# One chunk of a transformer block's attention sums its channel tiles further, with a new hand-written order and another place for late output tiles

## The chip, the cores and the metric

The kernel runs on one core of one Trainium2 chip. What counts is the device time of one execution in microseconds (us): 205.92 us is the median of three runs of the kernel before (205.92 to 206.48).

## What is computed

The reference normalizes `x` (2048 positions, 640 features, bf16) and adds to it an attention over a dilated window and a dense layer pair, both of the normalized `x`.

```python
def _A_ref(x, wqkv, wo):          # H = 32 heads of Dh = 20, W = 8, dil = 2
    qkv = (x @ wqkv).reshape(B, S, 3, H, Dh).transpose(2, 0, 3, 1, 4)
    q, k, v = qkv[0], qkv[1], qkv[2]
    idx = pos[:, None] - (jnp.arange(W) * dil)[None, :]
    mask = idx >= 0
    ...
    logits = jnp.einsum("bhsd,bhswd->bhsw", q, kg) * scale
    logits = jnp.where(mask[None, None, :, :], logits, -1e9)
    attn = _softmax(logits, axis=-1)
    o = jnp.einsum("bhsw,bhswd->bhsd", attn, vg)
    return o.transpose(0, 2, 1, 3).reshape(B, S, D) @ wo

def _B_ref(x, w1, b1, w2, b2):    # F = 1536
    h = _gelu(jnp.einsum("bsd,df->bsf", x, w1) + b1)
    return jnp.einsum("bsf,fd->bsd", h, w2) + b2

xn = _layernorm(x, axis=-1)
return x + _A_ref(xn, A_wqkv, A_wo) + _B_ref(xn, B_w1, B_b1, B_w2, B_b2)
```

Each position looks at itself and at seven positions before it, two apart. There are 32 heads with 20 channels each.

## The kernel before

The 2048 positions are four chunks (n = 0 to 3) of 512, each four blocks of 128 (j or bl = 0 to 3). The work is cut into named pieces, and `ORDER` (from line 42) is a list of their names, written out by hand: the pieces are issued in this order, and each engine executes its own in the order in which it meets them. No scheduler moves anything. A piece waits where its inputs, or the buffer it writes, are not ready; whatever is queued behind it on the same engine waits as well.

In the names the first digit is the chunk. The pieces of one chunk are:

- `st`, `rs`, `rc`, `xn`: statistics and normalization (`su`, `sq`, `ng` in chunks 2 and 3, where ScalarE makes the sums); `tc`: the normalized rows are transposed, from chunk 1 on by a transposing DMA on SyncE's queue (`do_td`, L295).
- `pj` and `pc`: projections to q, k and v by TensorE (L339) and their copies out of PSUM by ScalarE (L403). Chunk 0 has `ga`, `gd`, `hj` and `hc` instead. Two buffers serve the four chunks' v tiles, so a copy of chunk 2 waits until chunk 0 is done with its own.
- `qk` (L436): VectorE multiplies q with four shifted views of k, one half of the window at a time, 128 x 2560 elements. A partition holds one of four channel groups of one of 32 heads, and five channel tiles (t = 0 to 4) hold the rest.
- `pa` (L471): VectorE adds channel tiles: step 0 adds tiles 2 and 3 to tiles 0 and 1 (128 x 2048), step 1 adds tile 1 to tile 0, step 2 adds tile 4 to tile 0 (128 x 1024 each). `KEPT[n]` says how many tiles are left: 2 for chunk 0, where step 2 is left out, and 1 for the others.
- `lg` (L479): TensorE sums what is left over the four channel groups, with 32 output columns for each block, so that the four blocks' matmuls lie side by side in the array. These matmuls are called readers here, since they read what VectorE has made. There are 2 halves x 4 blocks x `KEPT[n]` of them.
- `cl`, `mask`, `m`, `mx`, `ex`, `ss`, `ri`, `at`: the softmax; `xd` (L554): its weights are broadcast by DMA, on SyncE's queue, to the four channel groups, one DMA for each block.
- `av` (L563): VectorE multiplies the shifted views of v with the weights; `aa` (L573): the two halves are added by a DMA with accumulation on GpSimd's queue (by VectorE, L575, in chunk 3); `ab` (L582) and `ot` (L586): the rest of the sum over the window, by VectorE.
- `f1` (L595) and `ge` (L611): first dense layer and GELU. In chunk 3 the results lie in the weights of q and k, which are spent by then (`do_ge`).
- `o` (L631 and L633): second dense layer (pieces 0 to 3) and the output projection of the attention (piece 4) into one pair of PSUM tiles, `lo` with 512 columns and `hi` with 128. `oc` (L638): ScalarE copies them to a tile `osb`, of which the pool `outp` has two. `od` (L644): a DMA on GpSimd's queue adds the tile to the output in DRAM.
- The output in DRAM first receives `x` (`xp`, SyncE's queue) and then the bias b2 (`xb`, GpSimd's queue, accumulating); an `od` waits until the `xb` of its chunk has landed. The very last block is finished otherwise (`oclo`, `ohi`, `ochi`, `ochd`): VectorE adds, and plain DMAs store.

Two lists name blocks whose `ab` or first `pa` would be done by a DMA (`AB_DMA`, `PA_DMA`); all their entries are empty.

Of the kernel before, what the change touches and what calls it, by code (L numbers as in the profile page):

```python
# [22 lines left out]
NCH = S // CH  # L23
BPC = CH // P
# [5 lines left out]
LASTB = S // P - 1  # L30
WARM = 10

KEPT = (2, 1, 1, 1)
BY_DMA = ((0, 1, 2, 3), (0, 1, 2, 3), (0, 1, 2, 3), ())
AB_DMA = ((), (), (), ())
PA_DMA = ((), (), (), ())
CUT = 2560
ACT_STATS = (2, 3)

# [3 lines left out]
wb st00a sum1 wa pad01 st00 rs00 ldx rc00 xn00a tp00a xn00b tp00b tc00a ga neg1 sq1 rs01 rc01 tc00b gb2 mean1 xn01  # L43
tp01 gb3 gb4 tc01a gd tc01b ho ge gc1 st03a st03 rs03 gc0 hj102 rc03 hc102 tb b1 hj101 hc101 st02a st02 rs02 hj100
hc100 xn03 tp03 tc03 pk hj202 rc02 xn02 tp02 tc02 gc4 hj201 hc201 hj111 st11a st10a hc111 st12a hj012 hc012 st11 hc202
st13a st13 hj112 hc112 st10 st12 rs1 qk010 rc1 qk000 qk011 hj110 f10_0 ge0_0 hj212 xn13 qk001 xn10 tc13 xn11 hc212
pa010 hj011 hj010 hc010 f10_11 f10_2 hc110 hc011 qk031 qk021 ge0_11 f10_10 qk020 pa000 su23 f10_6 xn12 ge0_10 qk030
pa020 su21 tc10 tc11 su22 hj200 hc200 f10_3 ge0_3 pa030 pa011 f10_9 tc12 xp0 su20 ng2 sq21 ge0_9 pa021 pj101 pc101
ge0_2 sq23 pj111 pj102 pj114 pc114 xp2 pc102 pj110 pc110 pj104 pa001 ge0_6 pa031 lg0 pc111 cl0 ldo xb3 xb2 pc104 mask
m0 mx0 ex0 pj112 pj103 pc103 pj113 pc113 ss0 ri0 pad11 pj100 pc100 pc112 qk121 qk120 hj211 sq20 hc211 qk101 ld2 pj124  # L50
qk100 sq22 pc124 f10_4 rs2 f11_6 pj121 rc2 ge0_4 pa120 qk110 f11_2 f10_1 ge0_1 pa121 qk111 xn21 pj123 pc123 ge1_6
pa122 pa100 pa110 xn23 f10_7 ge0_7 f11_8 tc23 f11_0 o000 xn20 tc20 tc21 ge1_2 f10_5 ge1_0 xb0 xn22 tc22 qk131 at0 xd00
ge1_8 f11_3 ge1_3 pa111 qk130 su32 pa101 pc121 f10_8 ge0_8 pad02 hj210 f11_5 pa130 pj120 pc120 pj200 pc200 pa112 pj211
pc211 pj210 pj212 pa131 pa102 pc210 hc210 pad12 pa132 lg1 av000 cl1 pj202 ge0_5 pj214 pc202 pj204 av001 aa00 m1 xd02
av021 pad21 av020 xd01 av011 av010 pj220 pj203 su33 ge1_5 su31 su30 ng3 sq33 xd03 av031 o001 pc212 pc203 o002 pc214
sq30 ab00 ot00 aa02 aa01 sq32 sq31 pj213 pc213 xp1 pj221 pj224 rs3 av030 ab02 pj122 pc122 pad22 rc3 ot02 o003 o004
oc00 od00 pj201 mx1 ex1 ss1 ri1 at1 xn31 pc220 xn30 f11_9 o020 o021 o022 o023 xd10 ab01 ot01 pc204 o024 oc02 pc201
aa03 tc30 ab03 f11_4 pc224 o030 o031 o032 pj223 o033 ot03 o034 xn33 av100 f12_3 av101 aa10 xn32 pc223 xd12 av120 xd13
f12_0 f11_11 av130 oc03 pc221 o010 o011 ge2_3 f12_11 o012 ge2_11 ge1_4 ge1_9 xd11 av110 av111 aa11 o013 o014 av121
pj222 pc222 av131 aa13 tc31 tc33 tc32 pj302 pj322 pj300 pc322 pj314 pc314 pj312 ab10 f11_1 ge1_11 ge1_1 f11_7 pj303  # L60
qk201 ot10 qk200 pa200 pc312 ge2_0 pj301 pc301 ab11 pa201 f11_10 pc302 ge1_10 qk211 ot11 od02 qk210 ab13 qk231 ot13
pj324 pc324 pj304 pc304 pa210 qk230 aa12 qk221 ab12 ge1_7 pj311 pa211 oc01 ot12 pa230 od01 f13_2 qk220 pc311 f12_8
pa212 od03 ge3_2 pa220 pc300 o130 pa231 pj313 pa221 o131 o132 o133 o134 oc13 pj310 f13_0 pc303 pc310 ge2_8 xb1 o120
pa202 pa232 pa222 lg2 o121 o122 pad31 pc313 qk300 f13_6 qk311 cl2 m2 qk310 f13_10 qk331 mx2 ge3_6 f13_8 qk330 ge3_0
f13_3 ge3_3 pa310 o123 qk301 o124 ex2 ss2 oc12 od12 f12_7 qk320 ri2 pa311 at2 xd23 pa330 pa300 qk321 f12_4 o110 o111
o112 pa301 o113 ge3_10 f12_10 pa320 pa312 o114 oc11 ge2_10 f12_6 f13_7 ge3_7 ge3_8 ge2_7 o100 o101 pa321 f12_2 xd21
od13 pa331 pa302 pa322 f12_5 o102 o103 ge2_6 ge2_5 o104 pa332 lg3 od11 oc10 od10 pj323 av210 pc323 av211 f12_9 cl3 m3
f13_1 xd22 xd20 ge3_1 pj321 av230 f12_1 ge2_1 aa21 av231 f13_5 ge3_5 av201 av200 aa23 f13_9 mx3 ge2_2 ge2_4 aa20 ab21
f13_4 ge2_9 ot21 ex3 ss3 ri3 ge3_4 f13_11 ge3_11 av220 ab23 o210 o211 at3 xd30 o212 o213 o214 ot23 oc21 od21 av221
aa22 pj320 o330 ab20 pc321 ot20 ge3_9 pad32 pc320 av300 o310 av301 o200 o201 o202 o203 o204 oc20 od20 o311 o230 o231  # L70
xd31 av310 o232 xd32 o233 o234 oc23 o312 o220 o221 o222 av311 aa31 ab22 ot22 o223 o224 od23 oc22 od22 av321 o313 av320
aa32 ab32 ot32 o320 o321 o322 o323 o324 oc32 od32 ab31 ot31 o314 oc31 od31 o300 xd33 o301 o302 o303 aa30 av331 ab30
ot30 o304 oc30 od30 av330 aa33 ab33 ot33 o331 o332 o333 o334 ohi xl oclo ochi ochd
""".split()


# [1 line left out]
def kernel(  # L78
# [16 lines left out]
    nc = tc.nc  # L95
# [19 lines left out]
    outp = ctx.enter_context(tc.tile_pool(name="outp", bufs=2))  # L115
# [3 lines left out]
    wqkv = [wts.tile([P, KT, D], BF16, name=f"w{s}_sb") for s in "qkv"]  # L119
# [60 lines left out]
    mask = consts.tile([H, W, MW], BF16, name="mask")  # L180
# [283 lines left out]
    def do_pa(n, j, k):  # L464

        a, b = ((slice(0, 2), slice(2, 4)), (slice(0, 1), slice(1, 2)), (slice(0, 1), slice(4, 5)))[k]
        kept, gone = (half[:, j, :, :, ts, :].rearrange("p h w t c -> p (h w) t c") for ts in (a, b))
        if k == 0 and j in PA_DMA[n]:
            nc.gpsimd.dma_start(kept, gone, accum_op=ALU.add)
            return  # L470
        nc.vector.tensor_tensor(out=kept, in0=kept, in1=gone, op=ALU.add)  # L471
# [104 lines left out]

    def do_ab(n, j):
        a, b = (half[:, j, 0, w : w + 2].rearrange("p w t c -> p (w t c)") for w in (0, 2))
        if j in AB_DMA[n]:
            nc.gpsimd.dma_start(a, b, accum_op=ALU.add)  # L580
        else:
            nc.vector.tensor_tensor(out=a, in0=a, in1=b, op=ALU.add)  # L582
# [33 lines left out]
    def do_o(n, bl, pc, parts):  # L616
# [11 lines left out]
        for k, (lhs, rhs) in enumerate(srcs):  # L628
# [3 lines left out]
            if "hi" in parts:  # L632
                nc.tensor.matmul(hi[:, 0 : D - CH], lhsT=lhs, rhs=rhs[:, CH:D], start=first, stop=last)  # L633

    def do_oc(n, bl):
        osb = outp.tile([P, D], BF16, tag="osb", name="osb")
        tiles["osb", n, bl] = osb
        nc.scalar.copy(osb[:, 0:CH], tiles["lo", n, bl][:])  # L638
        nc.scalar.copy(osb[:, CH:D], tiles["hi", n, bl][:, 0 : D - CH])  # L639
# [7 lines left out]
    last = (NCH - 1, BPC - 1)  # L647

    def do_oclo():
        osb = outp.tile([P, D], BF16, tag="osb", name="osb")  # L650
        tiles["osb", last] = osb
        nc.vector.tensor_tensor(out=osb[:, 0:CH], in0=tiles["lo", *last][:], in1=x_sb[:, LASTB, 0:CH], op=ALU.add)
        nc.sync.dma_start(out_sd[LASTB * P :, 0:CH], osb[:, 0:CH])
# [55 lines left out]
    for n in range(NCH):  # L709
# [87 lines left out]
```

## Time and profile before

| | |
|---|---|
| median of three runs | 205.92 us |
| the profiled execution | 206.31 us, of which the program's span is 204.5 |
| PE (TensorE matmul) busy | 200.3 us, 1261 matmuls |
| DVE (VectorE) busy | 181.6 us, 226 instructions |
| ACT (ScalarE) busy | 127.2 us, 246 instructions |
| POOL (GpSimd) busy | 34.6 us |
| granted clock of TensorE | full speed throughout |

The chain of work that ended last, in shares of the span, is

```profile
PE 75%; DVE 15%; DMA 5%; ACT 2%; issue 1%; SPq 1%; DVEq 0%; ACTq 0%
PE lo L631 23%; PE hps L595 20%; PE pps L339 17%; PE gps L383 7%; PE hi L633 6%; DVE half L436 5%; DVE half L471 5%; DMA x_sb<-e 3%; DVE half L563 3%; PE gps L352 1%; DVE half L582 1%; DMA x_sb<-in_A_x_dram 1%; PE L L479 1%; DVE oT L586 1%; PE tp L283 1%
```

It is followed back from the last instruction, at each step to what released it or to the instruction before it on its engine. L numbers are lines of the kernel printed above. PEld is the loading of weights, which overlaps the matmuls; names such as SPq are the queue of an engine, which issues DMAs. Rows with an arrow read: output, then inputs, then shape; "x16" counts instructions, and a bracket gives the idle time before the row and what ended it. The busy time of PE overstates its work, since rows of neighbouring matmuls overlap; the distance from start to start is the better measure.

### The profile page before, as it was taken

How to read it: one execution, taken by the hardware profiler on the slowest of the kernel's cores; microseconds unless marked ns; L12 is line 12 of the kernel's file. 1: busy time of each engine (PE TensorE's matmuls, PEld its weight loads, DVE VectorE, ACT ScalarE, POOL GpSimd, SP SyncE). 2: the span in 40 equal slices, each digit the busy share in tenths (PEclk: the TensorE clock that was granted, in tenths of full speed). 3: DMA queues.
4: the chain of work that ended last, by engine and by line, in shares of the span. 5: the costliest groups of instructions: out<-in, count | busy, mean ns of one | idle time of the engine just before them, and what ended most of it. 6: DMA issues, size and time to landing. Idle time of an engine off the chain costs nothing.

```text
span 204.5 us, 3231 instructions
## 1 busy us (share of the span) xinstructions
PE 200.3 (98%) x1261; PEld 111.4 (54%) x1261; DVE 181.6 (89%) x226; ACT 127.2 (62%) x246; POOL 34.6 (17%) x49
## 2 busy tenths in 40 slices
PE   8999999999999999999999999999999999999994
PEld 3898565564464555554554554455554455555552
DVE  2699999499998997877999999999989999889991
ACT  5589999999957998846335825474525793111210
POOL 2000000430000243002260050003104224111120
PEclk9999999999999999999999999999999999999999
DMA  6999469899358399999999086005642997962153
GB/s 208 392 396 380 109 213 328 306 256 199 78 116 275 67 171 163 163 144 151 192 190 189 6 90 105 0 0 69 130 107 32 169 189 127 216 101 25 27 67 64
DMA packets 27335, 31.77 MB, mean 155 GB/s; under 512 B 9272, under 2 KB 22072, under 8 KB 27320
## 3 DMA queue, kind: packets, MB, share of 16 engines
q0 software_dynamic: 7408, 12.78, 39.0%
q1 hardware_dynamic: 19600, 18.58, 31.8%
q8 instruction: 10, 0.16, 0.4%
q10 hardware_dynamic: 312, 0.20, 0.3%
q14 instruction: 5, 0.04, 0.1%
HBM read 10.00 MB, written 7.54 MB: 86 GB/s over the span
## 4 chain that ended last, share of the span: by engine, by line
PE 75%; DVE 15%; DMA 5%; ACT 2%; issue 1%; SPq 1%; DVEq 0%; ACTq 0%
PE lo L631 23%; PE hps L595 20%; PE pps L339 17%; PE gps L383 7%; PE hi L633 6%; DVE half L436 5%; DVE half L471 5%; DMA x_sb<-e 3%; DVE half L563 3%; PE gps L352 1%; DVE half L582 1%; DMA x_sb<-in_A_x_dram 1%; PE L L479 1%; DVE oT L586 1%; PE tp L283 1%
## 5 line engine op out<-in xcount | busy, mean ns | idle before, releaser
L595 PE MATMUL hps<-xnT,w_sb 128*128 128x512 bf16 x240 | 55.6, 379 | 0.0
L436 DVE TENSOR_TENSOR half<-qT,kT 128x2560 bf16<-128x2560 bf16 x32 | 46.6, 1483 | 0.1
L631 PE MATMUL lo<-w_sb,hT 128*128 128x512 bf16 x144 | 41.3, 379 | 0.0
L595 PEld LDWEIGHTS <-w_sb 128*128 128x128 bf16 x240 | 23.1, 98 | 26.2
L471 DVE TENSOR_TENSOR half<-half 128x1024 bf16<-128x1024 bf16 (+1 forms) x44 | 36.5, 878 | 0.0
L638 ACT CAST osb<-lo 128x512 bf16<-128x512 f32 x15 | 8.8, 583 | 37.1 <-PE hi L633 18.3
L633 PE MATMUL hi<-w_sb,hT 128*128 128x128 bf16 x144 | 31.5, 219 | 0.0
L611 ACT ACTIVATE hT<-hps,b1T 128x512 bf16<-128x512 f32 x36 | 24.0, 692 | 6.5 <-PE hps L595 5.6
L563 DVE TENSOR_TENSOR half<-vT,x_sb 128x2560 bf16<-128x2560 bf16 x16 | 23.0, 1487 | 3.3 <-DMA x_sb<-e 3.3
L644 POOL DMA_DIRECT2D out_dram<-osb x15 | 13.7, 959 | 71.8 <-ACT osb L639 71.8
L573 POOL DMA_DIRECT2D half<-half x12 | 15.6, 1302 | 56.1 <-DVE half L563 56.1
L563 DVE TENSOR_TENSOR half<-vT,ax 128x2560 bf16<-128x2560 bf16 x16 | 23.0, 1481 | 1.8 <-PE L L479 1.8
L631 PEld LDWEIGHTS <-hT 128*128 128x128 bf16 x144 | 14.1, 98 | 17.2 <-issue 0.4
L631 PE MATMUL lo<-wo,oT 128*128 128x512 bf16 x80 | 23.1, 379 | 0.0
L339 PE MATMUL pps<-xnT,wq_sb 128*128 128x512 bf16 x75 | 18.5, 379 | 0.0
L339 PE MATMUL pps<-xnT,wv_sb 128*128 128x512 bf16 x75 | 18.3, 379 | 0.0
L339 PE MATMUL pps<-xnT,wk_sb 128*128 128x512 bf16 x75 | 18.0, 379 | 0.0
L633 PE MATMUL hi<-wo,oT 128*128 128x128 bf16 x80 | 16.9, 219 | 0.0
L176 ACT ACT_TABLE_LOAD x12 | 15.4, 1283 | 0.9 <-PEq L781 0.7
L633 PEld LDWEIGHTS <-hT 128*128 128x128 bf16 x144 | 14.1, 98 | 1.9
L582 DVE TENSOR_TENSOR half<-half 128x1280 bf16<-128x1280 bf16 x16 | 13.1, 820 | 0.8 <-DMA half<-half 0.8
L403 ACT CAST vT<-pps 128x512 bf16<-128x512 f32 x15 | 8.8, 587 | 6.9 <-PE pps L339 6.9
(91 smaller groups left out, 262.9 us busy)
## 6 DMA issues: line engine op xcount, KB each, us to landing
half<-half POOLq DMA_DIRECT2D x12, 640.0 KB, 6.9
w_sb<-in_B_w_dram SPq DMA_DIRECT2D x4, 960.0 KB, 11.6
out_dram<-osb POOLq DMA_DIRECT2D x15, 160.0 KB, 3.5
ax<-e SPq DMA_DIRECT2D x8, 256.0 KB, 4.1
x_sb<-e SPq DMA_DIRECT2D x8, 256.0 KB, 4.8
out_dram<-b2bc POOLq DMA_DIRECT2D x3, 640.0 KB, 9.7
x_sb<-in_A_x_dram SPq DMA_DIRECT2D x1, 1280.0 KB, 13.7
out_dram<-x_sb SPq DMA_DIRECT2D x2, 640.0 KB, 4.4
```

The lines of the kernel that those rows point to most:

```text
L176: nc.scalar.activation(warm[:], nc.const_aps.tensor(0.0, [P, 1], F32), func)
L339: nc.tensor.matmul(ps[:], lhsT=wqkv_p[which][:, ti, to, :], rhs=xnT[:, ti, :], start=(ti == 0), stop=(ti == KT - 1),)
L383: nc.tensor.matmul(ps[:, to - a, :], lhsT=wqkv_p[which][:, ti, to, :], rhs=tiles["xnT", 0][:, ti, pair * 2 * P : (pair + 1) * 2 * P], star ...
L436: nc.vector.tensor_tensor(out=half[:, j, h], in0=q[:, :, at].unsqueeze(1).to_broadcast([P, W // 2, KT, P]), in1=window(k, h, at), op=ALU.mult,
L471: nc.vector.tensor_tensor(out=kept, in0=kept, in1=gone, op=ALU.add)
L563: nc.vector.tensor_tensor(out=half[:, j, h], in0=window(qkv_tile(n, 2), h, cs), in1=ax_view(n)[:, j, ws, :].unsqueeze(2).to_broadcast([P, ...
L573: nc.gpsimd.dma_start(a, b, accum_op=ALU.add, max_dma_last_dim=CUT)
L582: nc.vector.tensor_tensor(out=a, in0=a, in1=b, op=ALU.add)
L595: nc.tensor.matmul(ps[:], lhsT=w1_sb[:, ti, ft * P : (ft + 1) * P], rhs=tiles["xnT", n][:, ti, :], start=(ti == 0), stop=(ti == KT - 1),)
L611: nc.scalar.activation(hT, tiles["hps", n, ft][:], ACT.Gelu_apprx_tanh, bias=b1T[:, ft : ft + 1], scale=1.0)
L631: nc.tensor.matmul(lo[:], lhsT=lhs, rhs=rhs[:, 0:CH], start=first, stop=last)
L633: nc.tensor.matmul(hi[:, 0 : D - CH], lhsT=lhs, rhs=rhs[:, CH:D], start=first, stop=last)
```

## The change

Four things change.

1. `KEPT` becomes (1, 1, 1, 1). So chunk 0 has a third step of `pa` for each block (pieces `pa002`, `pa012`, `pa022`, `pa032`, four VectorE adds of 128 x 1024), and `lg0` has 8 matmuls instead of 16.
2. `ORDER` is another list. Its first lines, up to `hc202` and `st13a`, are the same; from there the pieces stand in another order. Among what moves: ten more `f1` matmuls stand ahead of `lg0`; ten fewer projection matmuls and three more lo/hi pairs stand between `lg1` and `lg2`; SyncE's queue in chunk 1 runs `xd10 xd12 xd13 tc31 xd11 tc33 tc32 tc30` instead of `xd10 tc30 xd12 xd13 xd11 tc31 tc33 tc32`; `xp1` stands ahead of chunk 2's transposes; of the bias adds only `xb0` is left early, `xb1` stands behind `od01`, `xb2` behind `od12` and `xb3` behind `od21`; `od20` and `od22` stand behind `od32`.
3. Output tiles of chunk 3, and the tile of chunk 2, block 0, are slices of the weights of v instead of tiles of the pool (`out_tile`). The pool keeps its two buffers for the others.
4. The two empty lists and the branches that read them are gone.

```diff
-KEPT = (2, 1, 1, 1)
+KEPT = (1, 1, 1, 1)
 BY_DMA = ((0, 1, 2, 3), (0, 1, 2, 3), (0, 1, 2, 3), ())
-AB_DMA = ((), (), (), ())
-PA_DMA = ((), (), (), ())
...
-st13a st13 hj112 hc112 st10 st12 rs1 qk010 rc1 qk000 qk011 hj110 f10_0 ge0_0 hj212 xn13 qk001 xn10 tc13 xn11 hc212
...
-oc00 od00 pj201 mx1 ex1 ss1 ri1 at1 xn31 pc220 xn30 f11_9 o020 o021 o022 o023 xd10 ab01 ot01 pc204 o024 oc02 pc201
-aa03 tc30 ab03 f11_4 pc224 o030 o031 o032 pj223 o033 ot03 o034 xn33 av100 f12_3 av101 aa10 xn32 pc223 xd12 av120 xd13
-f12_0 f11_11 av130 oc03 pc221 o010 o011 ge2_3 f12_11 o012 ge2_11 ge1_4 ge1_9 xd11 av110 av111 aa11 o013 o014 av121
-pj222 pc222 av131 aa13 tc31 tc33 tc32 pj302 pj322 pj300 pc322 pj314 pc314 pj312 ab10 f11_1 ge1_11 ge1_1 f11_7 pj303
...
+st13a st10 hj112 st13 st12 hj212 hc212 rs1 f10_3 ge0_3 qk000 rc1 xn11 xn10 tc10 xn13 hj110 hj011 hc011 tc11 qk010
...
+lg1 av000 su31 cl1 av001 pj202 f10_5 ge0_5 pj204 pc204 pc202 su33 aa00 pj214 pc214 ng3 sq31 xd02 av020 pj212 av021
+pc212 sq33 xd01 av010 pj223 av011 pj221 xd03 av030 ab00 ot00 av031 m1 pj220 pc220 pc223 aa02 ab02 ot02 f12_11 pc221
+o001 o002 o003 o004 oc00 aa01 mx1 ex1 ss1 pc121 pad22 ri1 at1 xd10 f12_0 ab01 sq32 sq30 rs3 xd12 rc3 ot01 o020 o021
+f11_10 aa03 ab03 od00 ot03 xd13 av100 o022 o023 o024 oc02 xn31 tc31 pj222 pj224 pc224 xn33 pc222 xd11 av101 aa10 o030
+o031 o032 o033 o034 xn30 oc03 tc33 pj201 o010 o011 o012 o013 pc201 ge1_1 av131 xn32 tc32 f12_8 av121 f12_4 ge2_4 o014
+av111 ge2_8 av130 f11_9 f11_11 ge2_11 ge2_0 tc30 pj314 av110 aa11 av120 pj303 pc303 ab10 ot10 pc314 pj304 pc304 qk201
...
+o331 o320 o321 o322 xd33 xd32 av321 av320 aa32 od21 ab32 ot32 o323 o324 oc32 xb3 od32 od20 ot31 aa30 o314 ab30 ot30
+od22 o300 av331 av330 o301 o302 o303 o304 oc31 aa33 od31 oc30 o332 o333 ab33 ot33 o334 oclo ohi ochi od30 ochd
...
+    def out_tile(n, bl):
+        if (n, bl) == (2, 0) or n == NCH - 1:
+            return wqkv[2][:, bl if n == NCH - 1 else BPC, :]
+        return outp.tile([P, D], BF16, tag="osb", name="osb")
+
     def do_oc(n, bl):
-        osb = outp.tile([P, D], BF16, tag="osb", name="osb")
+        osb = out_tile(n, bl)
...
     def do_oclo():
-        osb = outp.tile([P, D], BF16, tag="osb", name="osb")
+        osb = out_tile(*last)
```

More of the change, by code (lines that the diff above doesn't have):

```diff
@@ L45 @@
 hc100 xn03 tp03 tc03 pk hj202 rc02 xn02 tp02 tc02 gc4 hj201 hc201 hj111 st11a st10a hc111 st12a hj012 hc012 st11 hc202
-st13a st13 hj112 hc112 st10 st12 rs1 qk010 rc1 qk000 qk011 hj110 f10_0 ge0_0 hj212 xn13 qk001 xn10 tc13 xn11 hc212
-pa010 hj011 hj010 hc010 f10_11 f10_2 hc110 hc011 qk031 qk021 ge0_11 f10_10 qk020 pa000 su23 f10_6 xn12 ge0_10 qk030
-pa020 su21 tc10 tc11 su22 hj200 hc200 f10_3 ge0_3 pa030 pa011 f10_9 tc12 xp0 su20 ng2 sq21 ge0_9 pa021 pj101 pc101
-ge0_2 sq23 pj111 pj102 pj114 pc114 xp2 pc102 pj110 pc110 pj104 pa001 ge0_6 pa031 lg0 pc111 cl0 ldo xb3 xb2 pc104 mask
@@ L50 @@
[L50 to L54, printed above, removed]
@@ L55 @@
-av021 pad21 av020 xd01 av011 av010 pj220 pj203 su33 ge1_5 su31 su30 ng3 sq33 xd03 av031 o001 pc212 pc203 o002 pc214
-sq30 ab00 ot00 aa02 aa01 sq32 sq31 pj213 pc213 xp1 pj221 pj224 rs3 av030 ab02 pj122 pc122 pad22 rc3 ot02 o003 o004
-oc00 od00 pj201 mx1 ex1 ss1 ri1 at1 xn31 pc220 xn30 f11_9 o020 o021 o022 o023 xd10 ab01 ot01 pc204 o024 oc02 pc201
-aa03 tc30 ab03 f11_4 pc224 o030 o031 o032 pj223 o033 ot03 o034 xn33 av100 f12_3 av101 aa10 xn32 pc223 xd12 av120 xd13
-f12_0 f11_11 av130 oc03 pc221 o010 o011 ge2_3 f12_11 o012 ge2_11 ge1_4 ge1_9 xd11 av110 av111 aa11 o013 o014 av121
@@ L60 @@
-pj222 pc222 av131 aa13 tc31 tc33 tc32 pj302 pj322 pj300 pc322 pj314 pc314 pj312 ab10 f11_1 ge1_11 ge1_1 f11_7 pj303
[L61 to L73, printed above, removed]
+st13a st10 hj112 st13 st12 hj212 hc212 rs1 f10_3 ge0_3 qk000 rc1 xn11 xn10 tc10 xn13 hj110 hj011 hc011 tc11 qk010
@@ new lines @@
+hc110 hj010 qk001 qk011 pa000 hc112 hc010 pad11 qk020 f10_4 su23 qk021 tc13 f10_1 xn12 tc12 pa010 qk030 f10_2 f10_11
+ge0_2 qk031 xp0 su22 ge0_1 ge0_4 f10_9 ge0_9 hj211 hc211 f10_6 xp2 pa020 ldo xb0 pa011 pj110 su21 su20 ng2 pj101 ge0_6
+pj103 sq23 pa030 pc110 pa001 ge0_11 pc103 pa021 ld2 pa031 pc101 pj114 pa012 sq22 pc114 pj112 pc112 f11_5 ge1_5 pa022
+xp1 pj100 pa002 f11_0 pc100 ge1_0 pa032 lg0 pj104 pj113 cl0 mask m0 pc104 pj102 mx0 ex0 ss0 pc113 pj111 pc111 pc102
+qk131 qk121 qk111 sq20 pj123 pc123 qk100 f10_0 sq21 rs2 rc2 ri0 pj120 f11_6 ge1_6 qk110 f11_1 pj124 qk101 pa110 pc120
@@ new lines @@
+xn22 f10_10 ge0_10 tc22 pa100 ge0_0 qk130 at0 pc124 qk120 f10_8 xn21 xn23 pa111 pa120 pa130 hj210 hc210 tc21 f11_2
+xn20 tc20 pj122 pc122 pa121 ge0_8 f11_3 f11_8 ge1_8 hj200 pa101 pj121 ge1_2 hc200 pad12 f10_7 ge0_7 o000 ge1_3 pa112
+tc23 pj203 pc203 pj210 pc210 su32 pa131 pad21 pj213 pc213 pj200 pc200 pa102 su30 pj211 pc211 pa122 pa132 xd00 pad02
+lg1 av000 su31 cl1 av001 pj202 f10_5 ge0_5 pj204 pc204 pc202 su33 aa00 pj214 pc214 ng3 sq31 xd02 av020 pj212 av021
+pc212 sq33 xd01 av010 pj223 av011 pj221 xd03 av030 ab00 ot00 av031 m1 pj220 pc220 pc223 aa02 ab02 ot02 f12_11 pc221
@@ new lines @@
+o001 o002 o003 o004 oc00 aa01 mx1 ex1 ss1 pc121 pad22 ri1 at1 xd10 f12_0 ab01 sq32 sq30 rs3 xd12 rc3 ot01 o020 o021
+f11_10 aa03 ab03 od00 ot03 xd13 av100 o022 o023 o024 oc02 xn31 tc31 pj222 pj224 pc224 xn33 pc222 xd11 av101 aa10 o030
+o031 o032 o033 o034 xn30 oc03 tc33 pj201 o010 o011 o012 o013 pc201 ge1_1 av131 xn32 tc32 f12_8 av121 f12_4 ge2_4 o014
+av111 ge2_8 av130 f11_9 f11_11 ge2_11 ge2_0 tc30 pj314 av110 aa11 av120 pj303 pc303 ab10 ot10 pc314 pj304 pc304 qk201
+qk200 pa200 pa201 ab11 pa202 f11_7 pj302 pc302 pj312 pc312 ot11 ge1_7 pj300 pc300 qk211 pj322 pc322 qk210 aa12 qk221
@@ new lines @@
+ab12 od03 pj311 ge1_11 pj310 pa210 ot12 pa211 qk220 f11_4 aa13 ab13 qk231 oc01 ot13 pc311 pa220 f13_0 ge1_4 o130 pj324
+pc324 ge1_9 pj301 qk230 od01 o131 o132 ge1_10 o133 ge3_0 o134 oc13 pa212 f12_3 pa230 pj313 pc313 pa221 pc310 o120
+pa231 o121 pa222 pa232 lg2 pad31 pc301 qk300 qk310 xb1 cl2 m2 o122 f12_10 qk321 f13_9 f13_6 ge3_9 od13 o123 o124 oc12
+od12 xb2 f12_5 qk311 qk331 pa310 pa311 ge2_5 qk301 f13_8 ge2_10 f13_7 ge3_8 f13_3 o110 o111 qk320 o112 o113 o114 ge3_6
+mx2 ex2 pa300 pa301 pa312 ss2 oc11 qk330 ri2 at2 ge3_7 xd21 f13_2 o100 pa302 f13_11 ge3_11 xd20 pa330 ge2_3 pa320
@@ new lines @@
+f12_1 ge2_1 od02 o101 o102 f13_10 ge3_10 o103 o104 pa331 pa321 ge3_2 pa322 pa332 f12_2 lg3 av210 av211 xd23 av231
+av230 f12_9 od11 oc10 ge2_2 xl av200 od10 cl3 xd22 m3 mx3 av201 o210 f12_7 ge2_7 f12_6 ge2_6 aa21 ab21 ot21 f13_1
+ge3_1 ge2_9 ex3 ss3 av221 f13_5 ri3 at3 av220 o211 aa23 ab23 o310 aa20 ab20 ot20 pj320 pc320 pj321 o212 xd31 ge3_5
+f13_4 ge3_4 o213 o214 oc21 pj323 o200 o201 o202 ot23 o330 pc323 pc321 pad32 av311 av310 aa31 ab31 ge3_3 o311 xd30
+av300 av301 aa22 ab22 ot22 o203 o204 oc20 o312 o230 o231 o232 o233 o234 o313 oc23 od23 o220 o221 o222 o223 o224 oc22
@@ L467, in do_pa @@
         kept, gone = (half[:, j, :, :, ts, :].rearrange("p h w t c -> p (h w) t c") for ts in (a, b))
-        if k == 0 and j in PA_DMA[n]:
-            nc.gpsimd.dma_start(kept, gone, accum_op=ALU.add)
-            return
         nc.vector.tensor_tensor(out=kept, in0=kept, in1=gone, op=ALU.add)
@@ L578, in do_ab @@
         a, b = (half[:, j, 0, w : w + 2].rearrange("p w t c -> p (w t c)") for w in (0, 2))
[L579 to L582, printed above, removed]
+        nc.vector.tensor_tensor(out=a, in0=a, in1=b, op=ALU.add)
     def do_ot(n, j):
```

## The prediction

> **What bounds the kernel now.** I read the page's busy rows first, then the waits, then the timeline around the four places where PE reads what DVE has made (L479), then the chain of waits through the stretch where PE stood still, and last SyncE's queue in that stretch.
>
> ```profile
> PE 200.3 (98%) x1261; PEld 111.4 (54%) x1261; DVE 181.6 (89%) x226; ACT 127.2 (62%) x246; POOL 34.6 (17%) x49
> ```
>
> PE's timeline at the readers of chunks 0, 1 and 2 (start, duration, instruction, and in brackets the idle time before it):
>
> ```profile
> 35.58 1.05 PE L479 MATMUL L<-half,head_of 128*32 128x512 bf16 x16
> 36.55 0.63 PE L339 MATMUL pps<-xnT,wk_sb 128*128 128x512 bf16 x2
> ...
> 64.50 0.61 PE L479 MATMUL L<-half,head_of 128*32 128x512 bf16 x8
> 65.05 1.28 PE L339 MATMUL pps<-xnT,wq_sb 128*128 128x512 bf16 x5
> ...
> 127.13 0.39 PE L479 MATMUL L<-half,head_of 128*32 128x512 bf16 x2
> 127.70 0.61 PE L479 MATMUL L<-half,head_of 128*32 128x512 bf16 x6 [0.18 <-DVE half L471]
> ```
>
> A MATMUL's row is longer than its turn, so I go by starts: 512 columns follow each other at 0.216 us (five in 1.08), a lo/hi pair at 0.271 (126.49 to 126.76). By these pitches PE works without a gap from 5.7 us to its last matmul at 201.8, with two exceptions: about 0.1 before lg1, and 0.57 us at lg2 (127.13 to 127.70, of which the row shows 0.18, because the two matmuls before it still drain). So PE sets the end, and DVE is so close behind that it stops PE once. The chain of waits, cut to that stretch, says why:
>
> ```profile
> 89.43 6.99 DMA x_sb<-e
> 96.45 3.93 DVE half L563 x3
> ...
> 122.91 4.76 DVE half L471 x7
> 127.70 0.61 PE L L479 x6
> ```
>
> The broadcast of attention weights xd11 (L554) landed 7.0 us after its issue; DVE waited, and had not made it up when PE wanted the sums 31 us later. DVE's and SyncE's own rows there:
>
> ```profile
> 82.09 0.69 DVE L525 TENSOR_TENSOR sums<-e 128x512 f32<-128x512 bf16 x1 [1.46 <-ACT e L519]
> 89.38 5.79 DVE L563 TENSOR_TENSOR half<-vT,x_sb 128x2560 bf16<-128x2560 bf16 x4 [1.23 <-DMA x_sb<-e]
> 96.45 5.70 DVE L563 TENSOR_TENSOR half<-vT,x_sb 128x2560 bf16<-128x2560 bf16 x4 [1.29 <-DMA x_sb<-e]
> ```
>
> ```profile
> 85.31 0.55 SPq L554 DMA_DIRECT2D x_sb<-e  x1
> 85.97 2.12 SPq L295 DMA_TRANSPOSE xnT<-xn  x1
> 88.18 2.66 SPq L554 DMA_DIRECT2D x_sb<-e  x3
> 90.89 7.97 SPq L295 DMA_TRANSPOSE xnT<-xn  x3
> ```
>
> **The change, part by part.**
>
> *Fewer readers.* KEPT[0] 2 to 1 takes 8 of 16 matmuls out of lg0. They run side by side: 16 took 36.55 - 35.58 = 0.97 us, 8 took 65.05 - 64.50 = 0.55. Gain on PE: 0.42.
>
> *Four more adds.* pa002 to pa032, 128x1024, are the form that follows itself at 0.60 (119.28 to 119.88). DVE gets 2.40 us more, all ahead of lg0. Nothing hides this by itself; the order has to.
>
> *The order at lg0 and lg1.* Ahead of lg0 stand ten more f1 matmuls (45 against 35), 2.16 us: PE comes at 35.58 + 2.16 = 37.74. DVE's last add ended at 35.29, now at 37.69, and its result is seen 0.06 later: even, and I allow 0.1. At lg1 ten more projection matmuls stand ahead: 64.50 + 2.16 - 0.42 + 0.1 = 66.3. DVE ended at 64.38; plus 2.40 is 66.8, less what the wait for chunk 0's logits gives back (2.06 now; eight matmuls fewer bring the copy up to 0.42 earlier): 66.4. About 0.1 is lost, as much as before. I allow 0.05 more.
>
> *lg1 to lg2, where it is decided.* PE's work between the two readers was 180 matmuls of 512 and 85 pairs: 38.9 + 23.0 + 0.55 = 62.5 (trace 62.6). In the new order it is 170 and 88 pairs: 36.7 + 23.9 + 0.55 = 61.1. DVE's 63 instructions there are the same kinds: 16 L563 and 8 L436 at 1.41, 4 and 8 L471 at 1.14 and 0.60, 8 L582 at 0.74, 8 L586 at 0.41, softmax 4.0: 56.2. Before, DVE took 63.3 (64.38 to 127.65): 7.1 idle, of which five waits make 4.95 (0.71 for lg1, 1.46 for exp, 0.26 for the add DMA, 1.23 for xd10, 1.29 for xd11) and 2.1 are small gaps behind dependent instructions. Now DVE may idle 61.1 - 56.2 = 4.9, and some 0.3 more because the last reader starts that much after the first. Less the 2.1, 3.1 are left for waits. The first falls to about 0.2: the next multiply waits for lg1's first matmul alone, which no longer waits for the last add. The exp's rises to 1.8: on ACT three V copies of chunk 2 (0.49 each, waiting for chunk 0's last multiply, whose tile they overwrite), oc00 (0.66), the exp table (1.5 with its dummy) and the exp (1.0) follow that multiply, 4.6 in all, against 2.8 of DVE's own work behind it (maxima 1.0, ab02 0.74, ot02 0.5, subtraction 0.6). The add aa03 has landed by then. xd10's stays at 1.2. That is 3.2 with xd11 at nothing, so lg2 waits 0.0 to 0.3 in place of 0.57; I take 0.1.
>
> *xd11, the price that the trace doesn't show.* It was issued 4.15 us behind the end of at1 (85.28), and landed 11.1 behind it. Now SyncE's queue is xd10, xd12, xd13, tc31, xd11, tc33. Three broadcasts take 1.85; then the transpose tc31 waits for xn31, which ACT can end about 2.4 behind at1 (the square-root table 1.28, rs3, rc3, xn31 0.92). A transpose's issue took 1.25 in quiet stretches and 2.1 to 3.5 here. So xd11, queued behind it, goes out at 3.7 to 4.7, with tc33, tc32 and tc30 behind it and chunk 3's projections behind those. Landing takes 4.0 (xd10, xd12) to 7.0: 7.7 to 11.7 behind at1. DVE needs it as the fifth multiply: 4.05 + 4 x 1.41 = 9.7. I take 9.5: aa03 still moved its 640 KB until 86.78 before, 1.5 us into these broadcasts, and in the new order it is issued some 7.5 us ahead of at1's end against its 6.3 to land. Each us beyond 9.7 is a us at lg2, so the two ends are no wait and 2.0 us.
>
> By the Trainium skill (DMA: Bandwidth & Descriptors, Queues, rings and completion order) a semaphore increment lands only after every earlier write of the same DMA engine, so a broadcast behind a transpose lands no earlier than the transpose. Before, xd12 stood right behind tc30 and landed in 3.97, no worse than xd02's 4.05 with none ahead. If tc31 took tc33's 7.6 us the rule would put xd11 at 2.4 + 7.6 = 10.0 and add 0.3.
>
> *Output tiles and the b2 adds.* Tiles of chunk 3, and tile (2,0), go to slices of w_v, free after the last projection, which PE runs ahead of o204. In the trace these copies (L638) wait for PE, not for a buffer: od32 landed at 196.28, 1.5 before the copy at 197.81 that took its buffer. So the move gains nothing by itself; it lets od20 and od22 stand behind xb3 on POOL's queue, and without it od20's late issue would hold one of two buffers. xb3 and xb2 leave the stretch 38.5 to 52.4, where nothing waited for them; xp1, on SyncE, goes ahead of chunk 2's transposes instead of behind chunk 0's broadcasts, where nothing waited either. ACT's twelve table loads stay twelve. xb3 now goes out some 18 us ahead of PE's end; it took 7.3 to land, and od32, which must wait for it, is due 8 us ahead of the end: no wait. od30, last in that queue, lands about 1.0 behind PE's end (copy, issue, 3.4 to land), and the program ends 2.75 behind it (201.8 to 204.55). Price 0.
>
> *Sum:* -0.42 - 0.57 + 0.1 + 0.05 + 0.1 = -0.74. Span 204.5 to 203.8. The profiled execution took 206.31, 0.39 over the median 205.92, so I take the difference from the median: 205.2.
>
> **The rivals.**
>
> *The wait moves over.* xd11 lands 10.5 behind at1: 0.8 at lg2, the sum is 0.0 to +0.1, 206.0. For it: the queue behind is the same, and tc33 follows at once as tc31 did. Against: aa03 is out of the way.
>
> *Slower: the transpose holds xd11.* tc31 issues in 2.3 and xd11 again needs 7.0: 11.7 behind at1, 2.0 late. The sum is -0.74 + 2.0 = +1.3: 207.2. It decides from about 11.0, which is what the trace of before showed, though with a 2.1 us issue in the middle and aa03 in flight.
>
> *The tail.* Five output adds (od32, od20, od22, od31, od30) leave within 6 us. od32 and od31 landed 1.6 apart; at 2.5 the fifth lands 0.5 to 0.9 behind the present end of the chain, which gives 206.0. Against: little else moves there (64 GB/s in the last slice).
>
> *It doesn't do what it says:* true of the tiles, whose buffers nothing waits for; the time is the forecast's.
>
> **How the numbers follow.** A measurement of this kernel tells 0.3% (0.62 us) from no change. Forecast 0.47 (204.9 to 205.6; 0.36 of it below 205.3, 0.11 within); the wait moves over 0.20 (0.14 same, 0.06 slower); the transpose 0.26, slower; the tail 0.07 (0.03 same, 0.04 slower). Faster 0.36, same 0.28, slower 0.36. The floor is 204.9 (both gains, no new wait) and the transpose's case ends at 207.2; I take 204.8 to 207.2.
>
> **What would show it.** Right: lg0 in 0.55; lg2's eight matmuls starting within 0.3 of each other beyond their own pitch; no L563 row of chunk 1 waiting over 0.3 for xd11; PE's last matmul near 201.1; the last instructions still PE, DVE and the ACT-queue store. Wrong: a wait on x_sb<-e of 1 us or more near 97 with lg2 late by as much; PE waiting at o134 for oT ahead of lg2; L582 waiting for the add DMA; or a chain that ends in out_dram<-wv_sb.

## The result: 0.6% slower, and the profile after

| | before | after |
|---|---|---|
| median (range, runs) | 205.94 us (205.71 to 208.81, 22) | 207.11 us (206.66 to 209.58, 22) |
| ratio to before | | 1.0059, 95% interval 1.0047 to 1.0072 |
| profiled execution, its span | 206.31, 204.5 | 207.73, 205.8 |

The forecast was 205.2 (204.8 to 207.2), faster. The time lies inside the range, but on the other side of the kernel before, and none of the rivals that reach there happened as described. In the first two experiments below one execution each took over 300 us at a granted clock of 0.66 and is left out of the medians.

The busy row of the page of the changed kernel (this profile lacks 22 of the 1253 matmul records):

```profile
PE 199.9 (97%) x1231; PEld 111.8 (54%) x1253; DVE 184.1 (89%) x230; ACT 127.5 (62%) x246; POOL 34.7 (17%) x49
```

VectorE has 2.5 us more. TensorE's busy time can't be compared while records are missing; that it waits is read from its timeline at the three readers of chunks 0, 1 and 2 (start, duration, instruction), and at a place that the prediction doesn't mention:

```profile
28.31 1.24 PE L587 MATMUL hps<-xnT,w_sb 128*128 128x512 bf16 x5
30.23 1.03 PE L337 MATMUL pps<-xnT,wk_sb 128*128 128x512 bf16 x4 [0.68 <-DMA xnT<-xn]
...
38.96 0.62 PE L474 MATMUL L<-half,head_of 128*32 128x512 bf16 x8
39.51 1.27 PE L337 MATMUL pps<-xnT,wq_sb 128*128 128x512 bf16 x5
...
67.46 0.91 PE L474 MATMUL L<-half,head_of 128*32 128x512 bf16 x8
68.30 1.27 PE L337 MATMUL pps<-xnT,wq_sb 128*128 128x512 bf16 x5
...
129.02 0.74 PE L474 MATMUL L<-half,head_of 128*32 128x512 bf16 x8
129.70 0.39 PE L623 MATMUL lo<-w_sb,hT 128*128 128x512 bf16 x1
```

By starts, lg0 takes 0.55 in place of 0.97, as forecast. lg1 takes 0.84 (0.55 before), lg2 0.68 (1.12 before). And ahead of all of them, at the first projection of chunk 1, TensorE's five matmuls from 28.31 are done by pitch at 29.39 and the next one starts at 30.23: 0.84 lost, for a transposed tile of chunk 1. SyncE's queue there, first of the changed kernel, then of the kernel before:

```profile
21.98 6.94 SPq L293 DMA_TRANSPOSE xnT<-xn  x4
```

```profile
20.43 6.68 SPq L295 DMA_TRANSPOSE xnT<-xn  x4
```

Four transposes in both, but begun 1.55 later. About half of that is ScalarE, which ends the first normalized block of chunk 1 at 21.14 in place of 20.41. The rest is the queue. In the new order SyncE takes tc10 first, while ScalarE normalizes block 1 first (xn11 ends at 21.14, xn10 at 21.95): SyncE waits for xn10 with tc11's input ready behind it. Before, its order was tc13, tc10, tc11, tc12, and xn13 was first on ScalarE too.

xd11, on which the prediction hung its doubts, is on time. SyncE's queue and VectorE in that stretch, in the changed kernel:

```profile
88.55 2.48 SPq L549 DMA_DIRECT2D x_sb<-e  x3
91.14 2.06 SPq L293 DMA_TRANSPOSE xnT<-xn  x1
93.24 0.61 SPq L549 DMA_DIRECT2D x_sb<-e  x1
93.95 2.43 SPq L293 DMA_TRANSPOSE xnT<-xn  x1
```

```profile
92.25 7.10 DVE L558 TENSOR_TENSOR half<-vT,x_sb 128x2560 bf16<-128x2560 bf16 x5 [0.65 <-DMA x_sb<-e]
```

xd11 goes out at 93.24, 4.7 us behind the end of at1 (88.52), and lands at 97.62, 9.1 behind it. VectorE runs five multiplies through without a gap; the fifth, which needs xd11, starts at 97.86.

The end costs more as well: the program ends 3.13 us behind TensorE's last matmul (202.63 to 205.77), before 2.79 (201.76 to 204.55).

### The profile page after: what moved, and what is told of

The parts are those of the page before. It is cut to its first block, busy times and chain, and to the rows that moved or that the text cites. A ratio compares the mean times of both kernels' runs of the same rounds, so it can differ in the third digit from the quotient of the medians.

```text
span 205.8 us, 3191 instructions
## 1 busy us (share of the span) xinstructions
PE 199.9 (97%) x1231; PEld 111.8 (54%) x1253; DVE 184.1 (89%) x230; ACT 127.5 (62%) x246; POOL 34.7 (17%) x49
## 4 chain that ended last, share of the span: by engine, by line
PE 91%; ACT 4%; DMA 1%; issue 1%; DVE 0%
PE lo L623 27%; PE pps L337 24%; PE hps L587 21%; PE hi L625 8%; PE gps L381 5%; PE idle L447 2%; ACT xn L264 2%; PE gps L350 1%; PE L L474 1%; DMA xnT<-xn 1%; ACT trash L222 1%; ACT hT L603 1%; PE tp L281 1%; ACT qT L396 0%; ACT kT L396 0%
## 5 line engine op out<-in xcount | busy, mean ns | idle before, releaser
L587 PE MATMUL hps<-xnT,w_sb 128*128 128x512 bf16 x235 | 56.3, 379 | 0.3
L623 PE MATMUL lo<-w_sb,hT 128*128 128x512 bf16 x138 | 40.4, 379 | 0.0
L466 DVE TENSOR_TENSOR half<-half 128x1024 bf16<-128x1024 bf16 (+1 forms) x48 | 38.9, 862 | 0.2
L603 ACT ACTIVATE hT<-hps,b1T 128x512 bf16<-128x512 f32 x36 | 23.5, 688 | 8.9 <-PE hps L587 8.9
L623 PE MATMUL lo<-wo,oT 128*128 128x512 bf16 x77 | 22.6, 379 | 0.0
L641 POOL DMA_DIRECT2D out_dram<-osb x11 | 11.8, 1104 | 50.8 <-ACT osb L636 50.8
L635 ACT CAST osb<-lo 128x512 bf16<-128x512 f32 x11 | 6.5, 587 | 19.3 <-PE lo L623 10.9
L337 PEld LDWEIGHTS <-wk_sb 128*128 128x128 bf16 x75 | 8.7, 117 | 8.4 <-issue 1.1
```

What stands on the lines that cost most here:

```text
L337: nc.tensor.matmul(ps[:], lhsT=wqkv_p[which][:, ti, to, :], rhs=xnT[:, ti, :], start=(ti == 0), stop=(ti == KT - 1),)
L587: nc.tensor.matmul(ps[:], lhsT=w1_sb[:, ti, ft * P : (ft + 1) * P], rhs=tiles["xnT", n][:, ti, :], start=(ti == 0), stop=(ti == KT - 1),)
L603: nc.scalar.activation(hT, tiles["hps", n, ft][:], ACT.Gelu_apprx_tanh, bias=b1T[:, ft : ft + 1], scale=1.0)
L623: nc.tensor.matmul(lo[:], lhsT=lhs, rhs=rhs[:, 0:CH], start=first, stop=last)
L641: nc.gpsimd.dma_start(rows, tiles["osb", n, bl][:], accum_op=ALU.add)
```

## The experiments

The first theory, T, was: the loss is TensorE's wait at pj110, 0.3 at lg1 and 0.4 at the end, against gains of 0.42 at lg0 and some 0.5 at lg2. T2, in later expectations, is what the first four runs left of it. Medians beside these runs for the kernel before: 206.05 in the first and third group, 206.02 in the second.

**One transpose moved on SyncE's queue**

```diff
- ... rc1 xn11 xn10 tc10 xn13 hj110 hj011 hc011 tc11 qk010
+ ... rc1 xn11 tc11 xn10 tc10 xn13 hj110 hj011 hc011 qk010
```

> The changed kernel with one of chunk 1's transposes, tc11, moved on SyncE's queue to right behind xn11 (ahead of tc10, which waits 0.8 us for xn10 while tc11's input is ready). T (the loss is largely TensorE's wait at the first projections of chunk 1, 0.84 us at pj110, for transposes queued behind tc10): the wait falls below 0.3 and the time falls by 0.5 to 0.8 us, to 206.3 to 206.6. Rival R2 (the transposes are late because of what else the DMA engines move, not because of their order): tc12 lands at about 30 as before, the wait stays at 0.8 and the time at 207.1. Rival R1 (the loss lies with VectorE's four extra adds): VectorE's work is as late as ever, so what is won at pj110 is lost again as a longer wait at lg0 or lg1, and the time stays within 0.2 of 207.1.

207.11 us, ratio 1.0064 (1.0037 to 1.0090). T expected 206.3 to 206.6, and this looks like no gain at all, but the changed kernel itself did not run beside it, and there is no profile in which waits could be read. The swap is taken up again below.

**The tail of the new order in the old kernel**

```diff
- ... oc31 od31 o300 xd33 ... o304 oc30 od30 av330 aa33 ab33 ot33 o331 o332 o333 o334
+ ... oc31 od31 o331 o300 xd33 ... o304 oc30 od30 av330 aa33 ab33 ot33 o332 o333 o334
```

> The kernel before with one output tile's matmul group, o331, moved from behind o304 to ahead of o300, so that only two groups stand behind the last add on GpSimd's queue (as in the changed kernel) in place of three. TensorE's total work is the same. T (the end of the program is set by GpSimd's closing drain, which ends about 4.7 us after that queue's last issue, od30): od30 is issued 0.65 us later against TensorE's end, the gap from TensorE's last matmul to the program's end grows from 2.8 to 3.1 to 3.3, and the time rises by 0.3 to 0.5 us (206.2 to 206.4 against 205.9). Rival R3 (the end is set by the store behind TensorE's last tile or by the adds' landing): the gap stays at 2.8 and the time at 205.9.

206.39 us, ratio 1.0019 (1.0003 to 1.0034): +0.3, and the gap behind TensorE's last matmul is 3.10 (201.20 to 204.30). The closing instructions of four profiles, read from the records of the trace (us; SyncE's last wait is for the final stores):

```
                     PE's last  od30    od30    GpSimd's     SyncE's     program
                     matmul     issued  landed  drain ends   last wait   ends
before               201.76     198.86  202.25  203.57       203.72      204.55
after                202.63     200.34  203.68  205.00       204.58      205.77
o331 moved           201.20     198.95  202.20  203.52       203.17      204.30
before, once more    201.43     198.53  201.89  203.21       203.41      204.22
```

With od30 issued 2.9 ahead of TensorE's end the drain is done 0.15 to 0.2 before SyncE is; with 2.3 SyncE is done first, and the program ends 0.77 behind the drain. So T's number holds and R3's doesn't, but one sentence of T is too loose: the drain ends 4.5 to 4.7 behind od30's issue, and in all thirteen profiles of this case 1.32 behind its landing. The landing does count, 1.3 later than it seems to. By the Trainium skill (Perfetto Trace Analysis, Summary: the profiler window per engine type) the row of a DMA that GpSimd issues ends when its descriptors are made, not when data has moved; the trace agrees (od30's row ends 0.86 behind its start, its data lands 3.2 to 3.4 behind it).

**The new order without the four adds**

```diff
-KEPT = (1, 1, 1, 1)
+KEPT = (2, 1, 1, 1)
```

and pa002, pa012, pa022 and pa032 taken out of the order.

> The changed kernel with chunk 0's four extra adds taken out and 16 readers in lg0 again, all else in the new order. R1 (the loss lies with VectorE's four adds, 2.4 us of work ahead of lg0): lg0 costs 0.42 more, but the waits at lg1 and lg2 go, and the time falls by 0.5 us or more, to 206.6 or less. T (the adds fit; what was lost is at pj110 and at the end): lg0 costs 0.42 more, lg1's 0.3 of wait goes, and the time stays within 206.9 to 207.3.

207.45 us, ratio 1.0085 (1.0051 to 1.0118). R1 falls: without the adds the new order is no faster but, against the 207.11 of other runs, about 0.3 slower, a little above T's range too. lg1 still waits in its profile (0.82 by starts, 67.08 to 67.90), so that wait isn't the adds' doing, and with sixteen readers it can't be that of fewer readers either; the reason is taken up in the next section. At pj110 it shows 0.29, not 0.84.

**The four adds alone, in the old order**

```diff
-KEPT = (2, 1, 1, 1)
+KEPT = (1, 1, 1, 1)
...
- ... pj104 pa001 ge0_6 pa031 lg0 pc111
+ ... pj104 pa001 ge0_6 pa031 pa002 pa012 pa022 pa032 lg0 pc111
```

> The kernel before, in its old order, with chunk 0's four adds alone put in ahead of lg0 (8 readers). VectorE then ends its last add at about 35.3 + 2.4 = 37.7, where TensorE stands ready at 35.5. Both theories expect TensorE to wait 2.1 to 2.2 at lg0, to win 0.42 there, and VectorE to be late by up to 2.4 at lg1 and lg2 as well: time 207.6 to 208.3. If it came out at 206 or less, the new order would not have been needed at all and its cost would be the whole loss.

207.90 us, ratio 1.0115 (1.0074 to 1.0156), as both expected: lg0 waits for each of the four adds in turn, 2.2 us in all. The adds do need another order.

**The changed kernel once more**

> The changed kernel itself, profiled a second time. Its first profile came from an execution of 207.73 us, where the median is 207.11; the order that it shares with the sixteen-reader run waited 0.29 there at pj110 in place of 0.84. T2 (the loss is a row of small waits of the new order and 0.3 at the end; the 0.84 is a late landing of one execution): this profile shows 0.2 to 0.4 at pj110, and lg0 then 0.0 to 0.3 late on VectorE's pa032, lg1 0.2 to 0.3, lg2 up to 0.2, o320 0.18, and 0.3 at the end. T1 (the first reading: 0.84 at pj110 is the usual case and the largest part of the loss): pj110 waits 0.7 or more again.

207.21 us (ratio 1.0064, 1.0042 to 1.0085), the profiled execution 207.09 with a span of 205.3. TensorE at pj110:

```profile
28.24 1.24 PE L587 MATMUL hps<-xnT,w_sb 128*128 128x512 bf16 x5
29.75 1.03 PE L337 MATMUL pps<-xnT,wk_sb 128*128 128x512 bf16 x4 [0.27 <-DMA xnT<-xn]
```

28.24 + 1.08 = 29.32, so 0.43 is lost, a little more than T2 allowed, and tc12 landed at 29.62. In the first profile it was issued at 27.70 and landed at 30.09. T1 falls; the wait is usual, its 0.84 isn't. lg0 is not late here, lg1 0.29, lg2 0.10, o320 0.18 (it waits for the copy oc22), the gap at the end 3.18.

**The swap without the adds, and the swap again**

> The sixteen-reader kernel in the new order, with tc11 moved on SyncE's queue to right behind xn11, as in the first swap. There VectorE's last add is 2.3 us ahead of lg0, so nothing but the transposes holds TensorE ahead of it. T2: the 0.29 at pj110 goes, lg0, mask and the rest follow, and the time falls from 207.4 to 207.0 to 207.2. Rival R2 (order on the queue makes no difference, tc12 lands when it lands): 207.4.

> The changed kernel with tc11 right behind xn11, once more, beside the changed kernel on the same chip and with a profile. T2: pj110 waits less than 0.1, but VectorE's pa032 ends when it did, so that lg0 is 0.2 to 0.4 late instead, and the time is within 0.2 of the changed kernel's. R (the transposes cost all of what pj110 waits): lg0 isn't late and the time is 0.3 to 0.8 lower.

Without the adds: 207.11 us (1.0061, 1.0042 to 1.0081) against 207.45 without the swap (on another chip), and no wait at pj110: R2 falls, it was the order on the queue. With the adds: 206.84 us (1.0044, 1.0028 to 1.0061), against 207.21 on the same chip (1.0042 to 1.0085), and no wait at pj110 either. That the swap takes the wait away is shown; how much time it gives back isn't. By medians it is 0.3 to 0.4 in these two pairs, more than T2 allowed with the adds, but the intervals overlap, and the first group's 207.11 with the swap equals the changed kernel's 207.11 in the result. T2's reason is seen in the profile. TensorE and VectorE around lg0 with the swap (this execution's first weights landed 2 us late, which makes ScalarE's and VectorE's rows here 1.6 later):

```profile
38.45 1.24 PE L587 MATMUL hps<-xnT,w_sb 128*128 128x512 bf16 x5
39.62 0.76 PE L474 MATMUL L<-half,head_of 128*32 128x512 bf16 x7
```

```profile
34.50 5.43 DVE L466 TENSOR_TENSOR half<-half 128x2048 bf16<-128x2048 bf16 x8
```

VectorE's last add ends at 39.93, the reader of that block starts at 39.98, and the eight take 0.88 (39.62 to 40.50) in place of 0.55: in this execution part of what the transposes gave back is lost again here.

**xd11 ahead of the transpose tc31**

```diff
- ... xn31 tc31 pj222 pj224 pc224 xn33 pc222 xd11 av101
+ ... xn31 xd11 tc31 pj222 pj224 pc224 xn33 pc222 av101
```

> The changed kernel with the broadcast xd11 on SyncE's queue ahead of the transpose tc31 instead of behind it. The prediction's slower rival had this transpose hold xd11. T2: xd11 was no longer late in the changed kernel (landed 9.1 us behind at1, no wait), so putting it first changes nothing: within 0.2 of the changed kernel, and chunk 3's transposes, 0.6 to 0.8 us later, are waited for by nobody. Rival (xd11 and xd10's company still cost VectorE what lg2 waits): lg2's wait goes and the time falls by 0.2 to 0.4.

207.34 us (1.0069, 1.0050 to 1.0089), the changed kernel beside it 207.21. xd11 landed 7.4 behind at1 in place of 9.2, and nothing came of it: lg2 takes 0.66, as it did (0.65).

**The kernel before once more**

> The kernel before itself, profiled a second time. The prediction took 0.57 us at lg2 off the median, from a profile of 206.31 us where the median is 205.9. T2 (that stall belonged to one late landing of xd11 in that execution; the two variants of the kernel before showed none): this profile shows lg2 without a wait, VectorE waiting less than 0.3 for xd11, and if its time is near the median its span is 203.8 to 204.2. Rival (the stall is usual): 0.4 or more at lg2 again.

The profiled execution took 205.99, with a span of 204.2, and the stall at lg2 is not there. VectorE at xd10 and xd11, and TensorE at lg2:

```profile
89.63 5.84 DVE L563 TENSOR_TENSOR half<-vT,x_sb 128x2560 bf16<-128x2560 bf16 x4 [1.19 <-DMA x_sb<-e]
95.89 2.89 DVE L563 TENSOR_TENSOR half<-vT,x_sb 128x2560 bf16<-128x2560 bf16 x2 [0.42 <-DMA x_sb<-e]
```

```profile
127.37 0.62 PE L479 MATMUL L<-half,head_of 128*32 128x512 bf16 x8
127.92 0.39 PE L631 MATMUL lo<-w_sb,hT 128*128 128x512 bf16 x1
```

xd11 took 6.2 us from issue to landing in place of 7.0. VectorE waited 0.42 for it in place of 1.29, a little more than T2's 0.3, and ended its last add 0.3 ahead of lg2. The four other profiles of the old order show 0.00 at lg2 as well (o331 moved, the adds alone, this one, and the next): only the one that the prediction was made from has it.

**The output tiles alone, in the old kernel**

```diff
-        osb = outp.tile([P, D], BF16, tag="osb", name="osb")
+        osb = out_tile(n, bl)
```

> The kernel before with the output tiles alone: chunk 3's four and chunk 2's first lie in the slices of w_v, all else in the old order. The prediction priced this at 0, since the copies into these tiles wait for TensorE and not for a buffer. Every theory here expects the time of the kernel before within 0.2 (205.8 to 206.1); if it were slower by 0.3 or more, the place of the tiles would be part of the loss.

206.11 us, ratio 1.0014 (0.9998 to 1.0031): nothing that can be told from no change. The new order with two buffers in place of these tiles wasn't tried.

**The swap, and one add moved**

```diff
- ... qk001 qk011 pa000 hc112 hc010 pad11 qk020 f10_4 su23 qk021 tc13 f10_1 xn12 tc12 pa010 qk030
+ ... qk001 qk011 pa000 hc112 hc010 pad11 pa010 qk020 f10_4 su23 qk021 tc13 f10_1 xn12 tc12 qk030
```

> The swapped kernel (tc11 right behind xn11) with one of VectorE's adds, pa010, moved ahead of qk020, which waits 0.4 to 0.5 us for an evacuation by ScalarE while pa010's inputs are ready. T2 (with the transposes out of the way, VectorE's last add pa032 is what makes lg0 0.3 late, and VectorE carries that wait along): VectorE ends pa032 0.3 to 0.4 earlier, lg0 isn't late, lg1's wait stays at 0.2 to 0.4 because VectorE between lg0 and lg1 is no shorter, and the time falls by 0.1 to 0.3 against the swapped kernel's 206.84, to 206.5 to 206.7. Rival (VectorE isn't what holds lg0): no change.

206.66 us, ratio 1.0031 (1.0018 to 1.0044). TensorE at lg0 and lg1:

```profile
37.97 0.61 PE L474 MATMUL L<-half,head_of 128*32 128x512 bf16 x8
38.52 1.27 PE L337 MATMUL pps<-xnT,wq_sb 128*128 128x512 bf16 x5
...
66.46 0.91 PE L474 MATMUL L<-half,head_of 128*32 128x512 bf16 x8
67.30 1.27 PE L337 MATMUL pps<-xnT,wq_sb 128*128 128x512 bf16 x5
```

lg0 is back at 0.55, lg1 stays at 0.84. The time can't be told from that of the swap alone (1.0028 to 1.0061), but it lies clear below the changed kernel's in the result (1.0047 to 1.0072): about half of the loss is undone by two moves, each of one piece, that touch no arithmetic. What stays is lg1 (0.29), the end (0.43), o320 (0.18), lg2 and lg3 (0.08 and 0.15), less lg0's 0.42: 0.7 by these rows, 0.6 by the medians (206.66 - 206.05). No version that ran is faster than the kernel before.

## Why the prediction was wrong

**The step that failed first: "0.57 us at lg2 (127.13 to 127.70 ...)", put into the sum as "- 0.57", and "I take the difference from the median".** The stall was real, but it was part of one execution of 206.31 us, 0.39 above the median. Five profiles of the old order, one with it and four without, show that the median hasn't got it. A gain of 0.57 was taken off a time that did not contain the loss. Without this term the prediction's own sum is -0.74 + 0.57 = -0.17: no change. That the time still lies inside the range is luck: the upper end is the price of a late xd11, and xd11 was on time.

**The step that was not there: SyncE's queue ahead of lg0.** The prediction went through that queue at xd11 and mentions `xp1`, but not chunk 1's transposes; its sentence on the stretch ahead of lg0 counts f1 matmuls and VectorE's adds only. The transposes were reordered against ScalarE's order of normalizing, and of the four profiles of the new order without the swap, pj110 waits 0.29 to 0.49 for them in three and 0.84 in one. The swap shows the cause: with it the wait is gone. What it costs is read from these rows.

**The step on lg1: "About 0.1 is lost, as much as before. I allow 0.05 more."** It measured 0.29. The sum there counted on the copy cl0 coming "up to 0.42 earlier". It came not at all earlier. ScalarE around it, in the second profiles of the changed kernel and of the kernel before:

```profile
38.59 0.69 ACT L603 ACTIVATE hT<-hps,b1T 128x512 bf16<-128x512 f32 x1 [0.49 <-PE hps L587]
39.18 1.06 ACT L487 CAST Lb<-L 128x512 bf16<-128x512 f32 x2
40.34 0.58 ACT L401 CAST qT<-pps 128x512 bf16<-128x512 f32 x1
```

```profile
35.91 0.59 ACT L403 CAST kT<-pps 128x512 bf16<-128x512 f32 x1
36.49 1.07 ACT L492 CAST Lb<-L 128x512 bf16<-128x512 f32 x2
37.45 0.60 ACT L403 CAST qT<-pps 128x512 bf16<-128x512 f32 x1
```

lg0 starts at 38.48 and 35.83, so cl0 starts 0.70 behind it with eight readers and 0.66 with sixteen, each time right behind the evacuation in front of it on ScalarE. (Not all of the 0.42 was there to be won: the first of cl0's two copies reads the first half's readers alone, and these end 0.40 behind lg0's start with eight and 0.61 with sixteen.) VectorE's way from lg0's first matmul to its last add ahead of lg1 is then as long as ever: 38.48 to 67.24 is 28.76, 35.83 to 64.63 is 28.80. TensorE's way between the same readers is 28.50 (38.48 to 66.98) in place of 28.92: shorter by the 0.42 of the fewer readers. So 0.29 of that gain is given back at the next reader. That the evacuation is what holds cl0 is read from these rows; no run moved it.

But it isn't all that holds VectorE. With sixteen readers in the new order TensorE's way is 28.92 again, and lg1 is late all the same: VectorE's way has grown to 29.17 (38.15 to 67.32). ScalarE there:

```profile
40.44 0.59 ACT L401 CAST qT<-pps 128x512 bf16<-128x512 f32 x1 [0.53 <-PE pps L337]
42.45 1.04 ACT L514 ACTIVATE e<-Lb 128x1024 bf16<-128x1024 bf16 x1
```

The first row is pc104, which stands between cl0 and the exp in both orders. In the old order its matmuls, pj104, stand ahead of lg0, and it follows cl0 without a wait; in the new order they stand behind lg0, and it waits 0.53 for them with sixteen readers and 0.10 with eight. The exp starts 4.30 behind lg0's first matmul with sixteen (38.15) and 3.87 with eight, against 3.85 in the kernel before. So the new order costs VectorE at the exp what the fewer readers win there. With eight readers two ways to the exp end at the same time, cl0 with VectorE's maxima and subtraction behind it, and pj104 with pc104 and the exp's table load behind it. By these rows, moving one of the two alone would win little; neither move was tried.

**The step on the end: "od30 ... lands about 1.0 behind PE's end, and the program ends 2.75 behind it ... Price 0".** The landing was forecast rightly (203.68, 1.05 behind). But GpSimd's drain ends 1.32 behind that landing and the program 0.77 behind the drain, which makes 3.1 in place of 2.8; the run with o331 moved shows this cost by itself. The prediction held the landing against TensorE's end and against the stores, and the drain stood in no view that it read; the rival of the tail took the same measure.

**What was right.** The fewer readers: 0.55, and going back to sixteen without the adds costs 0.3 of the 0.42 in the whole (207.45 against 207.11, in different groups of runs). The adds need another order: alone they cost 1.9 (207.90 - 206.05). xd11 behind tc31: forecast 9.5 behind at1 where VectorE needs it at 9.7, measured 9.1 and 9.2; moved ahead, no change. The prediction's sentence on the Trainium skill (DMA: Bandwidth & Descriptors, Queues, rings and completion order) is borne out as little as it is denied: tc31 landed 7.2 behind at1 in the second profile, 2.0 ahead of xd11, so the rule had nothing to hold. The output tiles: 0. lg2 at 0.1: 0.68 and 0.65, against 0.55 for eight readers that wait for nothing.

**The sum from the second profiles of both kernels** (spans 204.2 and 205.3): first projection of chunk 0 +0.10 (6.34 to 6.44, though the first weights landed no later; why is open), pj110 +0.43, lg0 -0.42, lg1 +0.28, lg2 +0.10, lg3 +0.13, o320 +0.18, the end +0.39 (2.781 to 3.175): +1.19, where the spans differ by 1.1 and the medians by 1.17.

What stays open: why the wait at pj110 is 0.29 in one execution and 0.84 in another. The issues of the four transposes took 1.2 to 2.2 us each in the two profiles of the changed kernel; what delayed which was not separated. Open as well is how much of the 0.29 at lg1 each of the two ways to the exp would give back.

## What to carry to other kernels

Before a stall of one profiled execution goes into a sum as a gain, set that execution's time against the median: where it lies above it by about the stall's size, the median may not contain the stall, and a second profile settles it. When an order is rewritten, go through every in-order queue against its producers' new order, also where nothing was waited for before; and ask of each shorter stage whether the next reader on the slower engine moves with it, since otherwise the gain is a wait one stage on, and what the new order has put behind that stage on the faster one. The end of a program is set by whichever engine closes last, so the last issue on each queue has a due time of its own.

## What was not expected of the hardware

GpSimd's closing drain ends 1.32 us behind the landing of the last DMA that GpSimd issued, in thirteen profiles. SyncE's last wait ends 1.94 to 1.98 behind TensorE's last matmul in twelve of them, so in this kernel that DMA costs nothing as long as it lands no more than 0.6 behind that matmul (1.94 less 1.32): 0.49 and 0.46 in the two profiles of the kernel before, 1.05 and 1.08 in those of the changed one.

The landing of the first weights (wq) varied between 5.8 and 7.9 us from the start over twelve profiles of the same loads; the execution with 7.9 took 208.44 us where the median of its kernel is 206.84. The next latest, 7.2, belongs to the execution of 208.13 (xd11 ahead of tc31, median 207.34).
